# Pacing by VectorE's work, one PSUM pool and an ordered tail in a gated attention and mixer kernel

## Chip, cores and metric

One core of one Trainium2 chip. The metric is the device time of one execution in microseconds (us). TensorE (PE, its weight loads PEld), VectorE (DVE), ScalarE (ACT) and GpSimd (POOL) compute; SyncE (SP), ScalarE and GpSimd also issue DMAs. Each engine works through its own queue in order.

## What is computed

All tensors are float32; S = 2048 tokens, D = 640 channels, 32 heads of 20, F = 1728.

```python
qkv = x @ wqkv                                   # 32 heads of 20
p = softmax((q @ k.T) * 20 ** -0.5)              # 2048 x 2048 for each head
a = concat_heads(p @ v) @ wo
h = layernorm(x)                                 # over channels
b = (gelu(h.T @ w1 + b1) @ w2 + b2).T            # mixing over the 2048 tokens
g = sigmoid((x * gate_w).sum(-1, keepdims=True))
out = g * a + (1 - g) * b
```

## The kernel before

To keep float32 accuracy, operands are split into a high part (rounded) and a low part (the rest), written `hi_lo` (line 38): a copy on one engine, a subtraction on another. A product is three matmuls, high x high, high x low and low x high. Everything runs in one function, in these stages:

1. **Projections** (lines 344 to 542). Ten matmuls on zeros warm PE up (`warm`, 344 to 348). `load_x` (336) loads and splits blocks of x, `load_w` (289) the weights of q and k, `qk_unit` (299) multiplies and stores a 128 x 512 block of q or k as high and low parts to DRAM (`q_d`, `k_d`); `kd_d` holds differences of two key columns. Two projection blocks come first, then v with the gate, then the other blocks. Their PSUM tiles come from `st_tile` (73), four single banks in the pool `four`.
2. **Mixer** (lines 545 to 747). `mlp` (661) is a generator that yields after each step of two matmuls on 64 rows each (`pair64`): for each half `d` of the channels 14 hidden blocks `u` (656 steps), then 16 output blocks `y` (640 steps), 2592 steps in all. Weights come through `w_raw`, `w_split` and `w_need` (474 to 512). Between the steps run the row maxima of the first 1082 of the 2048 + 2 score tiles: attention subtracts each row's maximum through two extra rows of the score matmul, so all scores are computed once for their maximum (`s_mm`, 187) and once for the exponential. For the first eight of the 16 head pairs eight tiles are handled together (`s_diff`, 230): three go through a ScalarE relu (`s_over`, 208) and are joined on VectorE by a custom operation (`s_two`, 219), two take a VectorE reduce (`s_one`, 202): five VectorE operations for eight tiles. For the later pairs (`s_raw`, 257) each tile takes its own reduce; the last 58 tiles of the mixer stage are of this kind. Two tiles are emitted when `done < S_AHEAD * (n + 1) / STEPS`, evenly over the steps (line 731). They use four PSUM banks (`s` twice, `s3`, `pv`), the mixer the four of `st_tile`.

   The order on ScalarE, VectorE, POOL and SP is that of the program. On ScalarE a planner (`act`, `settle`, `force`, lines 547 to 581) decides where an operation is emitted: each has a cost in ns, a delay from which it may start and a slack until it is due; the clock of the plan advances by 146 per step and 233 per two score tiles. While the second half's input is normalised (`h_norm`, 450, in the y blocks of d = 0), VectorE does this as well.
3. **Attention loop** (lines 749 to 921). 16 head pairs x 32 iterations. An iteration has four score matmuls (`st_mm`), one exponential on a pair of banks (`st_pair`, 867), two on single banks (`st_one`, 875), two more score tiles for maxima while some of the other 968 are left, and the products with v of the iteration before (`pv_flush`, 818). Its banks are those of `psum` and of a second pool `trio`, which opens when `four` closes. `pv_evac` (803) copies the result out and stores it (`o_d`) and the row sums (`l_d`) to DRAM from POOL; `norm` (795) loads the row sums of some heads (`rl`), takes reciprocals on VectorE and stores them, repeated for the 20 rows of a head, to `r_d`. For the last four heads this happens at the end of the loop.
4. **Tail** (lines 922 to 953). The rows of `o_d` and `r_d` are loaded, multiplied and split, the first four blocks of 128 rows in pieces of 256 columns (`o_early`, two of them in the last pair of the loop), the last block in pieces of 512 (`o_late`). For each of 16 token tiles the mixer's output is loaded from `y_d` (945), `a_mms` (930) does 24 matmuls with the first four blocks (a) and adds the gated result to it on VectorE (939). After all of them 6 matmuls per tile follow with the last block (b), the second addition and the store to `out` (953). These run on four banks of a pool opened after `trio` closes; ScalarE, VectorE, POOL and SP are here in an order of the compiler's choice.

Of the kernel before, what the change touches and what calls it, by code (L numbers as in the profile page):

```python
# [30 lines left out]
def gated_mix(ctx, tc, xT, x, wqk, wv0, wv1, wo, w1, w1t, b1, w2, b2, out):  # L31
# [38 lines left out]
    four = ExitStack()  # L70
    banks = [four.enter_context(tc.tile_pool(name="four", bufs=1, space=PSUM))]
# [212 lines left out]
    def w_dma(m):  # L284
        raw = p1.tile([P, NC, P], F32, tag="xr", bufs=2, name=f"wr{m}")
        nc.scalar.dma_start(raw, wqk[m])
        return raw
# [11 lines left out]
    def qk_unit(m, w, q):  # L299
        wh, wl = w  # L300
        ps = st_tile([P, 512], f"qk{m}_{q}")
# [33 lines left out]

    def load_x(q):
        for c in range(NC):
            raw = px.tile([P, 512], F32, tag="x", bufs=8, name=f"xr{c}_{q}")
            nc.sync.dma_start(raw, xT[c * P:(c + 1) * P, q * 512:(q + 1) * 512])
            hi_lo(xh[c][q], xl[c][q], raw, hi_eng=nc.scalar)  # L340
# [5 lines left out]
    wps = st_tile([P, 512], "warm_ps")  # L346
    for i in range(10):
        nc.tensor.matmul(wps, warm[:, :P], warm, start=(i == 0), stop=(i == 9))
    raws = {0: w_dma(0), NC: w_dma(NC)}
    w = {0: load_w(0, raws[0])}  # L350
    load_x(0)
# [51 lines left out]
    for half in range(2):  # L403
        wvh, wvl = wvs[half]
        width = HALF + 2 if half == 0 else HALF
        for t in range(NT):
            n = NT * half + t
            if n == NT - 2:
                for i in range(4):
                    stats_load(i)  # L410
            if n == NT:
                nc.vector.tensor_scalar_mul(negm, gs[:, :, 1], -1.0 / D)
            if n in (2, 4, 6, 8, 10):
                split_wv(1, n // 2 - 1)
            if n == 2 * NT - 4:
                w[2] = load_w(2)
            ps = st_tile([P, width], f"v{half}_{t}")
# [353 lines left out]
    four.close()  # L771
    trio = ExitStack()
    tp = trio.enter_context(tc.tile_pool(name="trio", bufs=1, space=PSUM))
# [20 lines left out]

    def norm(h0, h1, at):
        loads, recips, stores = norm_steps(h0, h1)
        for n, f in enumerate(loads + recips + stores):
            if at is None:
                f()
            else:  # L800
                later[at if n == 0 else at + 10 + 2 * n] = f

    def pv_evac(p, qh, pv):
        ev = ap.tile([P, 512], F32, tag="oev", bufs=2, name=f"oev{p}_{qh}")
        nc.vector.tensor_copy(ev, pv)  # L805
        for j in range(2):
            h = 2 * p + j
            for c in range(2):
                r = 32 * (2 * j + c) + 11 * j
                cols = slice(qh * 1024 + c * 512, qh * 1024 + (c + 1) * 512)  # L810
                nc.gpsimd.dma_start(o_d[DH * h: DH * h + DH, cols], ev[r: r + DH, :])  # L811
                nc.gpsimd.dma_start(l_d[h: h + 1, cols], ev[r + DH: r + DH + 1, :])
        if qh == 1 and p in (7, 11, 13, 15):
            norm({7: 0, 11: 16, 13: 24, 15: 28}[p], 2 * p + 2, None if p == NP - 1 else 32 * p + 38)
# [23 lines left out]
    o_hl = {}  # L838

    def o_part(q, rows, k, n, tag, bufs, hi_eng, lo_eng):  # L840
        def t(name, dt=F32):
            return ap.tile([P, k, n], dt, tag=name + tag, bufs=bufs, name=f"{name}{tag}{q}")
        raw, rb, oh, ol = t("or"), t("rb"), t("oh", F32R), t("ol", F32R)
        cols = slice(q * n, (q + 1) * n)
        nc.sync.dma_start(raw, o_d[rows].rearrange("(c p) s -> p c s", p=P)[:, :, cols])
        nc.sync.dma_start(rb, r_v[rows].rearrange("(c p) s -> p c s", p=P)[:, :, cols])
        nc.vector.tensor_mul(raw, raw, rb)
        hi_lo(oh, ol, raw, hi_eng=hi_eng, lo_eng=lo_eng)
        return [(oh[:, i], ol[:, i]) for i in range(k)]

    def o_early(q, hi_eng=nc.scalar, lo_eng=nc.vector):
        o_hl[q] = o_part(q, slice(0, (NC - 1) * P), NC - 1, 256, "e", 2, hi_eng, lo_eng)

    def o_late(q):
        return o_part(q, slice((NC - 1) * P, D), 1, 512, "l", 4, nc.scalar, nc.vector)[0]
# [11 lines left out]
    def st_pair(g):  # L867
        ps = tp.tile([P, 2, 512], F32, tag="two", bufs=1, name=f"st{g}_0")
# [6 lines left out]
    def st_one(g, j):  # L875
        n = (2 * g + j) % 3
        ps = (psum if n == 2 else tp).tile([P, 512], F32, tag=("one0", "one1", "s3")[n], bufs=1, name=f"st{g}_1{j}")
# [6 lines left out]
    for p in range(NP):  # L884
# [3 lines left out]
        for it in range(32):  # L888
# [14 lines left out]
            if p == NP - 1 and it in (20, 26):  # L903
                o_early(it // 26, nc.gpsimd, nc.gpsimd)
# [17 lines left out]
    ordered.close()  # L922
    lps.close()
    trio.close()
    banks[0] = ctx.enter_context(tc.tile_pool(name="late", bufs=1, space=PSUM))

    ep = ctx.enter_context(tc.tile_pool(name="ep", bufs=1, side="right"))
    tys = [ep.tile([P, 2, HALF], F32, name=f"oy{t}") for t in range(NT)]

    def a_mms(t, ps, ohl, cc, cs):  # L930
        passes = [z for k, (oh, ol) in zip(cs, ohl) for z in ((oh[:, cc], woh[k]), (oh[:, cc], wol[k]),
                                                              (ol[:, cc], woh[k]))]
# [4 lines left out]
        c = slice(t, t + 1)  # L937
        for i in range(2):
            nc.vector.scalar_tensor_tensor(tys[t][:, i], ps[i], g_t[:, c], tys[t][:, i], op0=OP.mult, op1=OP.add)  # L939

    last = []
    for t in range(NT):
        if t % 2 == 0 and t // 2 + 2 < NT // 2:
            o_early(t // 2 + 2)
        nc.sync.dma_start(tys[t].rearrange("p a b -> p (a b)"), y_d[t * P:(t + 1) * P, :])
        if t in (4, 6, 8, 10):
            last.append(o_late(t // 2 - 2))
        ps = [st_tile([P, HALF], f"a{t}_{i}") for i in range(2)]
        a_mms(t, ps, o_hl[t // 2], slice((t % 2) * P, (t % 2 + 1) * P), range(NC - 1))
    for t in range(NT):  # L950
        ps = [st_tile([P, HALF], f"b{t}_{i}") for i in range(2)]
        a_mms(t, ps, [last[t // 4]], slice((t % 4) * P, (t % 4 + 1) * P), [NC - 1])
        nc.scalar.dma_start(out[t * P:(t + 1) * P, :], tys[t].rearrange("p a b -> p (a b)"))
# [47 lines left out]
```

## Time and profile before

| | |
|---|---|
| runs | 1814.91, 1814.11, 1813.07 us, median 1814.11 |
| profiled execution | 1807.24 us |
| its span | 1804.9 us |
| granted TensorE clock, mean | 0.997 |
| projections | 0 to 218 us |
| mixer with the first maxima | 218 to 746 us |
| attention loop | 747 to 1721 us |
| tail | 1721 us to the end |

Rows of a stretch (`A:B`) give its length, then for PE, PEld, DVE, ACT and POOL the busy time and in brackets the count of instructions, then the granted clock, the busy share of the DMA engines and GB/s. Rows of a timeline give start, duration, engine, line, operation, output<-inputs, shape, count, and in square brackets the idle time of the engine before it with what ended it. Rows of the waits give the waiting engine, what it waited for, total, times, longest. Rows of the groups (`L880 ACT ...`) give count, busy time, mean ns of one, idle time before. Rows of DMAs give count, size of each and median us from issue to landing.

### The profile page before, as it was taken

The numbers are of one execution on the slowest core, as the hardware profiler recorded it, in microseconds if no ns is written. First come the engines' busy times: TensorE is split into PE (matmuls) and PEld (weight loads), VectorE is DVE, ScalarE is ACT, GpSimd is POOL, SyncE is SP. The second block draws the span as 40 slices with busy tenths as digits, with TensorE's granted clock in tenths as the row PEclk, the third lists the DMA queues.
The fourth block names the chain that finished last, engine by engine and source line by source line (L and its number), as shares of the span: only waits on it lengthen the run. The fifth ranks groups of instructions, "written<-read, shape, count | busy, mean of one in ns | idle before, by whom it ended". The sixth has DMA issues, their size and how long they took to land. (4 is left out here: it accounts for less than half of the span.)

```text
span 1804.9 us, 39919 instructions
## 1 busy us (share of the span) xinstructions
PE 1787.0 (99%) x14978; PEld 1117.5 (62%) x14978; DVE 1240.6 (69%) x2407; ACT 1483.9 (82%) x2535; POOL 641.8 (36%) x898
## 2 busy tenths in 40 slices
PE   9999999999999999999999999999999999999998
PEld 7998799999999999533333333333333333333378
DVE  5303288899988888877767767676767677766136
ACT  4244378887888887699999999999999999999920
POOL 2113378788877777211110211121322121212210
PEclk9999999999999999999999999999999999999999
DMA  8657866556675564225222232052353332301463
GB/s 301 233 172 247 269 160 170 160 160 190 187 182 149 156 178 141 70 59 135 59 53 58 62 90 61 18 113 62 62 122 69 72 71 53 73 14 23 134 223 135
DMA packets 155666, 222.96 MB, mean 124 GB/s; under 512 B 65998, under 2 KB 92382, under 8 KB 152046
## 3 DMA queue, kind: packets, MB, share of 16 engines
q1 hardware_dynamic: 135472, 186.78, 38.2%
q0 software_dynamic: 15104, 23.01, 5.4%
q10 hardware_dynamic: 4896, 10.62, 1.8%
q8 instruction: 118, 1.93, 0.5%
q14 instruction: 76, 0.62, 0.1%
HBM read 165.43 MB, written 54.54 MB: 122 GB/s over the span
## 5 line engine op out<-in xcount | busy, mean ns | idle before, releaser
L205 DVE TENSOR_REDUCE mx<-s 128x1 f32<-128x512 f32 x1280 | 833.7, 687 | 288.9 <-PE s L199 225.1
L880 ACT ACTIVATE p<-st 128x512 f32<-128x512 f32 x1024 | 585.1, 659 | 0.0
L872 ACT ACTIVATE p<-st 128x1024 f32<-128x1024 f32 x512 | 553.8, 1082 | 1.3 <-PE st L865 0.7
L824 PE MATMUL pv<-p,v 128*32 128x512 f32 x4096 | 548.5, 605 | 0.1
L865 PEld LDWEIGHTS st<-qs_True,ks_True 62*128 62x128 f32 x2048 | 246.2, 185 | 434.9 <-ACT p L872 428.7
L865 PE MATMUL st<-qs_True,ks_True 62*128 62x512 f32 x2048 | 495.7, 446 | 1.8 <-ACT x L587 1.1
L199 PE MATMUL s<-ks_False,qs_False 60*128 60x512 f32 x1152 | 391.0, 398 | 4.5 <-ACT ov L214 2.9
L43 POOL TENSOR_TENSOR wl<-wr,wh 128x512 fp32r<-128x512 f32 x228 | 275.4, 1217 | 89.0 <-ACT wh L40 66.8
L224 DVE CUSTOM_DVE_ANT_0 ov<-s,ov 128x512 f32<-128x512 f32 x384 | 263.4, 687 | 38.6 <-PE s L199 24.9
L214 ACT ACTIVATE ov<-s 128x512 f32<-128x512 f32 x384 | 228.7, 597 | 73.0 <-PE s L199 61.9
L199 PE MATMUL s<-sk,sq 60*128 60x512 f32 x896 | 279.9, 394 | 0.0
L811 POOL DMA_DIRECT2D o_d<-oev x128 | 66.6, 521 | 590.4 <-DVE oev L805 587.9
L48 PE MATMUL y<-gh,wh 64*128 64x320 f32 x896 | 225.0, 309 | 0.0
L48 PE MATMUL u<-hl,wh 64*128 64x320 f32 x864 | 224.7, 307 | 0.0
L48 PE MATMUL u<-hh,wh 64*128 64x320 f32 x864 | 224.5, 307 | 0.0
L199 PEld LDWEIGHTS s<-ks_False,qs_False 60*128 60x128 f32 x1152 | 211.2, 185 | 14.7 <-DVE mx L205 6.7
L48 PE MATMUL y<-gl,wh 64*128 64x320 f32 x832 | 216.7, 307 | 0.0
L48 PE MATMUL y<-gh,wl 64*128 64x320 f32 x832 | 215.3, 306 | 0.0
L48 PE MATMUL u<-hh,wl 64*128 64x320 f32 x800 | 212.3, 307 | 0.0
L824 PEld LDWEIGHTS pv<-p,v 128*32 128x32 f32 x4096 | 83.1, 108 | 175.1 <-issue 162.6
L40 ACT ACTIVATE wh<-wr 128x512 fp32r<-128x512 f32 (+2 forms) x246 | 146.9, 600 | 52.7 <-DMA wr<-in_wqk_dram 22.5
L199 PEld LDWEIGHTS s<-sk,sq 60*128 60x128 f32 x896 | 166.3, 186 | 18.0
(130 smaller groups left out, 2441.3 us busy)
## 6 DMA issues: line engine op xcount, KB each, us to landing
wr<-in_w_dram SPq DMA_DIRECT2D x192, 256.0 KB
ks_True<-k_d SPq DMA_DIRECT2D x96, 160.0 KB
qs_True<-q_d SPq DMA_DIRECT2D x192, 80.0 KB
qs_False<-q_d SPq DMA_DIRECT2D x108, 80.0 KB
sk<-k_d SPq DMA_DIRECT2D x42, 160.0 KB
sq<-q_d SPq DMA_DIRECT2D x84, 80.0 KB
v_d<-vt SPq DMA_DIRECT2D x32, 168.0 KB
v<-v_d SPq DMA_DIRECT2D x16, 336.0 KB
```

Source lines behind the costliest of these rows:

```text
L40: nc.scalar.activation(hi, src, AF.Copy)
L43: (lo_eng or nc.vector).tensor_sub(lo, src, hi.bitcast(F32))
L48: nc.tensor.matmul(ps[k], a[r], b[r], start=start, stop=stop)
L199: nc.tensor.matmul(ps, qs[half][r, t * P:(t + 1) * P], ks[r, kc * 512:(kc + 1) * 512], start=True, stop=True)
L205: nc.vector.tensor_reduce(mx[:, slot, j, t: t + 1], ps, axis=AX.X, op=OP.max)
L214: nc.scalar.activation(over[j, kc], ps, AF.Relu)
L224: nc.vector.tensor_tensor_reduce(ov, ps, ov, 1.0, -3.0e38, OP.add, OP.max, mx[:, slot, j, t: t + 1])
L811: nc.gpsimd.dma_start(o_d[DH * h: DH * h + DH, cols], ev[r: r + DH, :])
L824: nc.tensor.matmul(pv[r: r + 32, :], v_tiles[p][:, kt, 10 * j: 10 * j + 32], pt[j, c], start=(kt == 0), stop=(kt == NT - 1))
L865: nc.tensor.matmul(ps, ks[r, kt * P:(kt + 1) * P], qs[qh][r, c * 512:(c + 1) * 512], start=True, stop=True)
L872: nc.scalar.activation(pt, ps, AF.Exp, scale=SCALE)
L880: nc.scalar.activation(pt, ps, AF.Exp, scale=SCALE)
```

## The change

- **Pacing.** Score tiles are emitted by VectorE's planned work: 435 ns for a tile of the first kind, 640 for the second, 400 for a normalisation. The sum grows evenly from step 14 on.
- **PSUM.** There is one pool: `s` twice, `s3`, `pv`, a pair of banks `two`, `one0`, `one1`. The projections rotate over the four single banks `s3`, `pv`, `one0`, `one1` (`one_tile`); mixer and tail take `two` and `one0`, `one1` in turn (`st_tile`); the loop uses the same tiles as before without opening a pool.
- **Opening.** Eight warm matmuls instead of ten; the first weight in two DMAs (one block, then four); the x blocks' DMAs ahead of the second weight's, which goes to POOL's queue.
- **Weight splits.** The splits 4 to 7 of the mixer's weights get a delay of 4000 ns and a slack of 2000.
- **Loop's end.** `pv_evac` issues the four `l_d` stores before the four `o_d` stores. In the last pair y is loaded by SP (`y_load`, one tile an iteration from the 13th on, into buffers that the loop's operands left), and four early pieces of `o_d` and `r_d` at the iterations 16, 20, 26 and 30.
- **Tail.** It keeps the program's order on all engines. Tiles 0 to 7 take the four first blocks (24 matmuls); each of tiles 8 to 15 takes all five (30), followed by the last block of the tile eight before it (6). The row sums of the last heads are loaded at the end of the loop, their reciprocals and stores come after tile 2, the late rows' multiplications at tiles 6 and 9; the late loads are issued by POOL, the stores to `out` by SP.

```diff
     def st_tile(shape, name):
         n = st_count[0] % 4
         st_count[0] += 1
-        return banks[0].tile(shape, F32, tag=f"st{n}", bufs=1, name=name)
+        if n == 0:
+            st_pair_of[0] = psum.tile([P, 2, 512], F32, tag="two", bufs=1, name=name)
+        if n < 2:
+            return st_pair_of[0][:, n, :shape[1]]
+        return psum.tile(shape, F32, tag=f"one{n - 2}", bufs=1, name=name)
+
+    def one_tile(shape, name):
+        n = one_count[0] % 4
+        one_count[0] += 1
+        return psum.tile(shape, F32, tag=("s3", "pv", "one0", "one1")[n], bufs=1, name=name)
...
-    for i in range(10):
-        nc.tensor.matmul(wps, warm[:, :P], warm, start=(i == 0), stop=(i == 9))
-    raws = {0: w_dma(0), NC: w_dma(NC)}
-    w = {0: load_w(0, raws[0])}
-    load_x(0)
+    for i in range(8):
+        nc.tensor.matmul(wps, warm[:, :P], warm, start=(i == 0), stop=(i == 7))
+    wr0 = p1.tile([P, NC, P], F32, tag="xr", bufs=2, name="wr0")
+    parts = (slice(0, 1), slice(1, NC))
+    for c in parts:
+        nc.scalar.dma_start(wr0[:, c], wqk[0][:, c])
+    xr0 = [x_dma(c, 0) for c in range(NC)]
+    raws = {NC: w_dma(NC, nc.gpsimd)}
+    w = {0: tuple(q4([P, NC, P], F32R, f"w{n}0") for n in "hl")}
+    for c in range(NC):
+        if c < 2:
+            hi_lo(w[0][0][:, parts[c]], w[0][1][:, parts[c]], wr0[:, parts[c]], hi_eng=nc.scalar)
+        x_split(c, 0, xr0[c])
...
-            act(lambda: w_split(j), 520, 0, 2200 * (j - k) - 4000)
+            act(lambda: w_split(j), 520, 4000 if j < 2 * AHEAD else 0, 2000 if j < 2 * AHEAD else 2200 * (j - k) - 4000)
...
+    FIRST = 14
+    U_STEPS = (FT - 1) * 48 + 32
+    DIFF, RAW, NORM = 435, 640, 400
+
+    def dve_work(k):
+        return DIFF * min(k, NDIFF * 128) + RAW * max(0, k - NDIFF * 128)
+
+    def dve_room(n):
+        norms = min(max((n - U_STEPS) / (NT * 40), 0), 1) * NT * NORM
+        return (dve_work(S_AHEAD) + NT * NORM) * (n + 1 - FIRST) / (STEPS - FIRST) - norms
...
-        while done + 2 <= S_AHEAD and done < S_AHEAD * (n + 1) / STEPS:
+        while done + 2 <= S_AHEAD and dve_work(done) < dve_room(n):
...
-                nc.gpsimd.dma_start(o_d[DH * h: DH * h + DH, cols], ev[r: r + DH, :])
                 nc.gpsimd.dma_start(l_d[h: h + 1, cols], ev[r + DH: r + DH + 1, :])
+                stores.append((o_d[DH * h: DH * h + DH, cols], ev[r: r + DH, :]))
+        for a in stores:
+            nc.gpsimd.dma_start(*a)
...
+            if p == NP - 1:
+                last_norm.extend(norm_steps(h0, H))
+                last_norm[0][0]()
...
-            if p == NP - 1 and it in (20, 26):
-                o_early(it // 26, nc.gpsimd, nc.gpsimd)
+            if p == NP - 1:
+                if it in (16, 20, 26, 30):
+                    e_load((16, 20, 26, 30).index(it))
+                if 13 <= it < 13 + NT:
+                    y_load(it - 13)
+                if it in (20, 26):
+                    e_high(it // 26, ap, nc.gpsimd)
+                    e_low(it // 26, nc.gpsimd)
...
+    late_args = {n: l_load(n) for n in (2, 0, 3, 1)}
+    for n in (2, 0, 3, 1):
+        nc.gpsimd.dma_start(*late_args[n][0])
+    e_high(2, lp)
     for t in range(NT):
+        q = t // 2 + 2
+        if t % 2 == 0 and 2 < q < NT // 2:
+            e_high(q, ap if q % 4 < 2 else lp)
+        lates = {NT // 2 - 2: (2, 0), NT // 2 + 1: (3, 1)}.get(t, ())
+        for n in lates:
+            l_high(n)
+        evacs = [a_tile(t, range(NC) if t >= NT // 2 else range(NC - 1))]
+        if t >= NT // 2:
+            evacs.append(a_tile(t - NT // 2, [NC - 1]))
+        for f in evacs:
+            f()
+        if t % 2 == 0 and q < NT // 2:
+            e_low(q)
+            if q + 2 < NT // 2:
+                e_load(q + 2)
+        for n in lates:
+            l_low(n)
+        if t == 2:
+            for f in last_norm[1] + last_norm[2]:
+                f()
+            for n in (2, 0, 3, 1):
+                nc.gpsimd.dma_start(*late_args[n][1])
+    ordered.close()
+    lps.close()
```

`e_load`, `e_high` and `e_low` are the load, the multiplication with the high part, and the low part of an early piece; `l_load`, `l_high` and `l_low` those of a late one. `a_tile` emits a tile's matmuls and returns its evacuation.

More of the change, by code (lines that the diff above doesn't have):

```diff
@@ L851, in o_early, with o_tiles @@
[L851 to L855, printed above, removed]
+    o_raw, o_hl, l_hl = {}, {}, {}
+    def o_tiles(q, k, n, tag, bufs, names, pool, dt):
+        if pool is lp:
+            return [lp.tile([P, k, n], dt, tag="sq", bufs=4, name=f"{name}{tag}{q}") for name in names]
+        return [pool.tile([P, k, n], dt, tag=name + tag, bufs=bufs, name=f"{name}{tag}{q}") for name in names]
@@ L867, in st_pair @@
     def st_pair(g):
[L868 removed]
+        ps = psum.tile([P, 2, 512], F32, tag="two", bufs=1, name=f"st{g}_0")
         for j in range(2):
@@ L921, in gated_mix, with a_tile @@
     pv_flush()
[L922 to L932, printed above, removed]
+    def a_tile(t, cs):
+        ps = [st_tile([P, HALF], f"a{t}_{cs[0]}_{i}") for i in range(2)]
+        passes = []
+        for k in cs:
+            (oh, ol), n, i = (o_hl[t // 2], 2, k) if k < NC - 1 else (l_hl[t // 4], 4, 0)
+            cc = slice((t % n) * P, (t % n + 1) * P)
+            passes += [(oh[:, i, cc], woh[k]), (oh[:, i, cc], wol[k]), (ol[:, i, cc], woh[k])]
         for i, (a, b) in enumerate(passes):
@@ L950, in gated_mix, with evac @@
[L950 to L953, printed above, removed]
+        def evac():
+            c = slice(t, t + 1)
+            for i in range(2):
+                nc.vector.scalar_tensor_tensor(tys[t][:, i * HALF:(i + 1) * HALF], ps[i], g_t[:, c], tys[t][:, i * HALF:(i + 1) * HALF], op0=OP.mult, op1=OP.add)
+                if t == NT // 2 - 1 and NC - 1 in cs:
+                    put = (nc.scalar if i else nc.sync).dma_start
+                    put(out[t * P:(t + 1) * P, i * HALF:(i + 1) * HALF], tys[t][:, i * HALF:(i + 1) * HALF])
+            if t != NT // 2 - 1 and NC - 1 in cs:
+                nc.sync.dma_start(out[t * P:(t + 1) * P, :], tys[t])
```

104 lines of the change are left out of this document (65 added, 39 removed).

## The prediction

> **What bounds the kernel now.** The first view is the page's head.
>
> ```profile
> span 1804.9 us, 39919 instructions
> PE 1787.0 (99%) x14978; PEld 1117.5 (62%) x14978; DVE 1240.6 (69%) x2407; ACT 1483.9 (82%) x2535; POOL 641.8 (36%) x898
> ```
>
> TensorE (PE) looks full. But its busy time comes from matmuls that overlap, and the count in equal stretches says more. The second view gives stretches of 22 us of the mixer stage (about 218 to 746 us), then one of them for the score tiles alone, then four rows of PE's timeline.
>
> ```profile
> 218.00:240.00 22.00, 19.15 (x208) 18.45 (x209) 14.66 (x35) 14.07 (x27) 11.57 (x11) 0.92 0.65 194
> 394.00:416.00 22.00, 21.89 (x265) 21.30 (x263) 20.86 (x52) 18.07 (x37) 18.14 (x20) 1.00 0.65 187
> 438.00:460.00 22.00, 21.67 (x266) 21.08 (x263) 20.55 (x52) 17.73 (x36) 19.03 (x21) 1.00 0.47 147
> 636.00:658.00 22.00, 22.00 (x276) 21.93 (x275) 19.25 (x50) 18.16 (x35) 15.07 (x18) 1.00 0.53 152
> 702.00:724.00 22.00, 21.74 (x251) 20.03 (x249) 20.58 (x45) 11.87 (x24) 15.56 (x18) 1.00 0.38 114
> 724.00:746.00 22.00, 21.68 (x217) 17.35 (x213) 22.00 (x38) 6.17 (x11) 7.42 (x8) 1.00 0.05 17
> ```
>
> ```profile
> 636.00:658.00 22.00, 15.76 (x48) 8.67 (x48) 19.01 (x30) 10.51 (x18) 1.00 0.53 152
> ```
>
> ```profile
> 742.71 0.31 PE L48 MATMUL y<-gh,wl 64*128 64x320 f32 x1
> ...
> 743.15 0.31 PE L48 MATMUL y<-gh,wl 64*128 64x320 f32 x1
> ...
> 745.68 0.31 PE L48 MATMUL y<-gh,wh 64*128 64x320 f32 x1
> 747.11 0.73 PE L865 MATMUL st<-qs_True,ks_True 62*128 62x512 f32 x3 [1.12 <-ACT x L587]
> ```
>
> The first bracket in a row is PE's count. A full stretch holds 276, which is 12.5 per us. Against that the first stretch lacks 68 matmuls (5.4 us), the last two lack 25 and 59 (6.7 us), and the three from 394 to 460 (first and last shown) lack about 11 each (2.6 us). Elsewhere in this stage little is missing. From 742.71 to 743.15 lie six intervals, so one mixer matmul takes 0.073 us and a step of two 0.147 us. The full stretch has 228 of them and 48 score tiles, which leaves (22 - 228 x 0.0733) / 48 = 0.11 us for a score tile.
>
> Next, why these stretches are short:
>
> ```profile
> PE s L199 <- ACT ov L214: 2.9, 1, 2.9
> ```
>
> ```profile
> 222.51 0.63 ACT L40 ACTIVATE wh<-wr 128x512 fp32r<-128x512 f32 x1 [1.72 <-DMA wr<-in_w_dram]
> 223.05 1.76 ACT L214 ACTIVATE ov<-s 128x512 f32<-128x512 f32 x3
> ```
>
> ```profile
> 224.00:228.00 4.00, 4.00 (x34) 4.00 (x32) 2.46 (x7) 1.83 (x4) 1.78 (x2) 0.58 0.98 310
> ```
>
> At the stage's start PE waits 2.9 us for a relu of a score tile. ScalarE runs in order, and that relu stands behind a weight split that waits for its DMA. After this pause the granted clock is 0.58 over 4 us, which costs 0.42 x 4 = 1.7 us more. Together: 4.6 us.
>
> ```profile
> 405.25 0.68 DVE L224 CUSTOM_DVE_ANT_0 ov<-s,ov 128x512 f32<-128x512 f32 x1
> ...
> 408.34 0.25 DVE L160 TENSOR_REDUCE mm<-mx 128x8 f32<-128x24 f32 x2
> ...
> 719.54 27.55 DVE L205 TENSOR_REDUCE mx<-s 128x1 f32<-128x512 f32 x46
> ```
>
> Where VectorE (DVE) is never idle, five operations take 408.34 - 405.25 = 3.09 us; these serve eight score tiles of the first kind (three take the relu's way), 0.386 us a tile. Of the second kind, from 719 us on, every tile needs its own reduce: 27.55 / 46 = 0.599 us. Before, both kinds come at 1082 / 2592 = 0.417 tiles a step. The 58 of the second kind then span 139 steps, in which PE needs 139 x 0.147 + 58 x 0.11 = 26.8 us and VectorE 34.7. VectorE is the bound there, and the missing 6.7 us are this.
>
> The attention loop is paced by ScalarE:
>
> ```profile
> L880 ACT ACTIVATE p<-st 128x512 f32<-128x512 f32 x1024 | 585.1, 659 | 0.0
> L214 ACT ACTIVATE ov<-s 128x512 f32<-128x512 f32 x384 | 228.7, 597 | 73.0 <-PE s L199 61.9
> ```
>
> No idle time stands before its exponentials, two of them single tiles in each of 512 iterations. Nothing in the change shortens them. Last the tail, by PE's timeline, stretches, the end of the chain, then VectorE, GpSimd (POOL) and SP:
>
> ```profile
> 1721.70 0.56 PE L935 MATMUL a<-woh,ohe 128*128 128x320 f32 x2
> ...
> 1750.18 1.09 PE L935 MATMUL a<-woh,ohe 128*128 128x320 f32 x2 [1.77 <-DVE oy L939]
> ```
>
> ```profile
> 1750.00:1754.00 4.00, 3.80 (x14) 3.55 (x15) 2.63 (x5) 0.00 (x0) 0.00 (x0) 0.57 0.82 281
> 1754.00:1784.00 30.00, 30.00 (x206) 29.91 (x205) 18.72 (x30) 5.57 (x7) 0.00 (x0) 1.00 0.19 63
> ```
>
> ```profile
> 1783.96 15.51 PE b L935 x95
> ```
>
> ```profile
> 1721.80 0.69 DVE L805 COPY oev<-pv 128x512 f32<-128x512 f32 x1 [12.67 <-PE pv L824]
> ...
> 1738.64 0.55 DVE L785 RECIPROCAL rl<-rl 128x64 f32<-128x64 f32 x1 [5.22 <-DMA rl<-l_d]
> ...
> 1748.43 1.23 DVE L847 TENSOR_TENSOR ore<-ore,rbe 128x1024 f32<-128x1024 f32 x1 [5.19 <-DMA ore<-o_d]
> ...
> 1784.78 15.72 DVE L939 SCALAR_TENSOR_TENSOR oy<-b,g_t,oy 128x320 f32<-128x320 f32 x32
> ```
>
> ```profile
> 1732.04 0.57 POOL L782 DMA_DIRECT2D rl<-l_d x1 [5.23 <-DMA l_d<-oev]
> 1739.49 2.75 POOL L789 DMA_DIRECT2D r_d<-rl x4 [6.89 <-DVE rl L785]
> ```
>
> ```profile
> 1740.30 0.37 SPq L846 DMA_DIRECT2D rbe<-r_d x1
> ```
>
> PE has 480 matmuls to do from 1721.70 on. At 30 / 205 = 0.1463 us that is 70.2 us, so they could end at 1791.9; they end at 1799.5. The 7.6 us go to two waits of VectorE for DMAs (5.2 us each), behind which PE runs out of banks, to a clock of 0.57 after the second, and to the b part, where 32 evacuations of 0.49 us set the pace (15.5 us for 95 matmuls, not 13.9).
>
> **The change part by part.**
>
> *Pacing.* VectorE's work is spread evenly over 2578 steps, the first 14 left free: 1024 x 435 + 58 x 640 + 16 x 400 = 488,960 ns, or 190 a step. That is 0.436 tiles a step of the first kind, 0.413 while the normalisations run (10 ns a step off), 0.296 of the second kind. The 58 late tiles now span 196 steps: PE 28.8 + 6.4 = 35.2 us, VectorE 34.7. Nearly level; I leave 1.0 us lost of 6.7: **-5.7**. In the dense stretches a step takes PE 0.147 + 0.436 x 0.11 = 0.195 us and VectorE 0.436 x 0.386 = 0.168, so PE stays the bound, with less air than before (0.161 of 0.193). I take **+1.5** (bounds 0, and 13.6 at the loss of 394 to 460: 33 matmuls of 828, so 4%, of 1742 steps or 339 us). In the normalising stretch 1% fewer tiles on an engine at its limit: **-1.0** (0 to -2.6).
>
> *Start of the mixer.* The free steps let the last projection banks drain, the new rotation begins on a bank pair that no projection used, and the first four splits get a delay of 4 us, so the first relus stand ahead of the split that waits for its DMA. PE meets the first split chunk of the new kind only at step 48, some 9 us in. **-4.6** (0 to -5.4).
>
> *One PSUM pool.* Before, the loop's first scores wait 1.12 us until the mixer's last bank is read, as a pool closes. Now they go into the pair that was read one tile earlier, but their exponential still stands behind the two evacuations on ScalarE: **-0.7** (0 to -1.1). The pair is freed only when both halves are read, half a microsecond after the first; a whole unit lies between, which hides it.
>
> *The opening.*
>
> ```profile
> 1.44 4.63 PE L348 MATMUL warm_ps<-warm 128*128 128x512 f32 x10 [1.44 <-DVE warm L345]
> ...
> 7.02 0.50 PE L54 MATMUL qk<-xh,wh 128*128 128x512 f32 x1 [0.95 <-ACT xh L40]
> ```
>
> The first weight comes in two pieces and the x blocks ahead of the second weight, which moves to POOL's queue. PE waits 0.95 us before its first product; half of that is won: **-0.5** (-1.0 to +1.7, the price of one clock step as at 224). The Trainium skill, "TensorE: Matmul & The Clock Gate", "Why this matters for your kernels", asks for at least 4 us of matmuls before the clock is full; eight at 0.463 us are 3.7, and by it the first products could run at half clock, which would make the sum 1.7 us worse. In the trace the clock is already up behind ten; no run here shows eight. The same section lets gaps of up to about 3 us go unpunished; the 1.77 us at 1750 were followed by 0.57, so here the trace decides against it. "DMA: Bandwidth & Descriptors", "Issuing engines are not separate DMA queues", says that another queue saves issue time only; by that the opening wins nothing and the sum is 0.5 worse.
>
> *The tail.* y is loaded in the last pair, where ScalarE paces and SP has nothing else due, so the 16 loads are hidden; without that cover they would fill the queues as before. The evacuations of a and b interleave: 36 matmuls (5.3 us) against four evacuations (2 us), so the 1.6 us of the b part go. The late reciprocals still stand in VectorE's order behind tile 2 (about 1734.6). Their chain:
>
> ```profile
> L812 POOL DMA_DIRECT2D l_d<-oev x128 | 64.1, 501 | 2.6 <-issue 2.6
> ```
>
> ```profile
> l_d<-oev POOLq DMA_DIRECT2D x128, 2.0 KB, 2.6
> ```
>
> ```profile
> r_d<-rl POOLq DMA_DIRECT2D x32, 160.0 KB, 5.7
> ```
>
> The copy ends at 1722.5, four l_d stores of 0.5 us now go first (1724.8), land after 2.6 (1727.4), rl arrives 6.6 later as before (1734.0): no wait. r_d stores issue until 1738, land by 1743; the new wait is that VectorE at tile 6 multiplies the late rows, for which POOL's loads must land. At 4 us each (no row shows them on POOL; bounds 2.6, and 8.1 as from 1740.30 to 1748.43) that is about 1747.5; behind the multiplication stands the evacuation of tile 6, for which PE's tile 8 waits from 1749.9. It just fits; I leave 1.0 us. PE ends 7.6 - 1.0 us earlier, with the last evacuations and stores as long as before: **-6.6** (0 to -7.6).
>
> *Sum:* -0.5 - 4.6 - 1.0 + 1.5 - 5.7 - 0.7 - 6.6 = **-17.6**. The profiled execution took 1807.2 us (span 1804.9), so 1789.6 there; the median of the runs shown is 1814.1, 6.9 above, and the same gain gives **1796.5**.
>
> **The rivals.**
>
> *Late rows come late.* Arrivals as slow as in the old tail (l_d 5.2, rl 6.6, r_d 5.7, load 8.1): VectorE stands until about 1754, evacuates tile 6 by 1755.9, PE loses 6.0 and then 1.7 by the clock instead of 1.0: 1796.5 + 6.7 = **1803**. For it: the two 5.2 us waits. Against: those ran beside the y loads.
>
> *VectorE binds in the dense stretches.* Loss as at 394 to 460, 13.6 instead of 1.5: **1809**. Against: VectorE's 0.168 of 0.195.
>
> *The late tiles stay bunched*, if planned costs don't fit: 5.7 less, **1802**.
>
> *Slower: the loop.* Its tiles move to other banks of the one pool. If the exponentials read these more slowly, each of 512 iterations pays. From 17.6 / 512 = 34 ns an iteration on nothing is won, from 41 on it is slower by over 0.2%. Between the two single-tile rows above lie 62 ns (659 and 597 for one shape); one such step gives 1796.5 + 512 x 0.062 = **1828**. Against: tile shapes and order stay.
>
> *All waits go:* 1.0 + 5.4 + 2.6 + 6.7 + 1.1 + 7.6 = 24.4, **1790**.
>
> **How the numbers follow.** Forecast 0.63 (own range 1792 to 1800), late rows 0.13, dense stretches 0.09, bunched 0.03, loop 0.07, all gone 0.05. The range 1789 to 1806 leaves out the dense stretches and the loop, 0.16. About 0.2% (3.6 us) is what a measurement of this kernel tells from no change; faster by more: 0.63 + 0.13 + 0.05 + 0.03 and 0.05 of the 0.09, together 0.89; same 0.04; slower 0.07.
>
> **What would show it.** Right: about 276 matmuls in each 22 us after the first, no clock step near 224, VectorE near its limit but PE not short before the loop, b matmuls at 0.146 us, and no wait of PE for oy. Wrong: fewer than 270 from 240 to 350; the multiplication of late rows waiting past 1750; exponentials longer than 659 ns; a clock step behind eight warm matmuls.

## The result, and the profile after

The changed kernel took **1799.97 us** (median of 6 runs, 1797.92 to 1806.11); the kernel before, beside it on the same chip, 1813.75 us (6 runs, 1810.34 to 1815.16). The ratio is 0.9934, 95% interval 0.9914 to 0.9954. The forecast was 1796.5 us: the sign is right, and 13.8 of the 17.6 us of gain came. The profiled execution was the longest of the six, 1806.11 us with a span of 1803.8. So the two profiles differ by only 1.1 us of span, and stages have to be compared, not totals. The table cuts the span at the first matmul of each stage (read from the trace); "again" is a second profile of the same changed kernel (first experiment).

| us | before | after | again | forecast of the change |
|---|---|---|---|---|
| opening and projections | 218.4 | 225.4 | 221.2 | -0.5 |
| mixer | 528.7 | 522.6 | 518.8 | -10.5 |
| attention loop | 974.6 | 975.6 | 975.5 | 0 |
| tail | 83.2 | 80.2 | 80.1 | -6.6 |
| span | 1804.9 | 1803.8 | 1795.7 | -17.6 |

The page's head of the kernel after:

```profile
span 1803.8 us, 39867 instructions
PE 1782.3 (99%) x14976; PEld 1108.8 (61%) x14976; DVE 1232.8 (68%) x2392; ACT 1482.9 (82%) x2536; POOL 646.1 (36%) x907
```

The stretches of 22 us that the prediction read, in the kernel after, with the dense middle (460 to 702 us) in one row:

```profile
218.00:240.00 22.00, 19.31 (x172) 17.11 (x170) 10.66 (x22) 9.96 (x18) 7.73 (x6) 1.00 0.90 291
240.00:262.00 22.00, 20.76 (x249) 20.37 (x251) 17.80 (x45) 18.56 (x40) 14.77 (x15) 1.00 0.61 162
394.00:416.00 22.00, 21.51 (x264) 20.90 (x262) 20.12 (x49) 18.48 (x37) 16.09 (x17) 1.00 0.52 155
438.00:460.00 22.00, 22.00 (x269) 21.64 (x268) 20.41 (x52) 18.04 (x36) 19.11 (x22) 1.00 0.62 186
460.00:702.00 242.00, 240.38 (x2936) 238.42 (x2934) 217.21 (x549) 198.75 (x392) 184.17 (x195) 1.00 0.62 164
702.00:724.00 22.00, 22.00 (x278) 21.86 (x276) 20.50 (x46) 13.79 (x27) 16.04 (x18) 1.00 0.50 148
724.00:746.00 22.00, 22.00 (x281) 21.95 (x279) 21.79 (x36) 9.43 (x17) 14.25 (x14) 1.00 0.23 71
```

The last two rows are the forecast come true: 278 and 281 matmuls where 251 and 217 stood. VectorE is busy 21.79 of 22 us in the last one, at its limit and no longer behind it. The first two show what did not come as forecast: the stage starts 7 us later and still lacks matmuls. The waits of PE, with the total, the number and the longest:

```profile
PE s L208 <- ACT ov L223: 5.2, 3, 2.3
PE a L1022 <- DVE oy L1028: 2.9, 8, 1.2
PE qk L54 <- DVE evl L43: 2.1, 1, 2.1
...
PE v L54 <- DVE kf L326: 1.1, 1, 1.1
```

The wait for the relus (`ov`) at the mixer's start has not gone, and eight waits for `oy` stand in the tail, where the kernel before had two (3.0 us). The tail's end, by the chain that ended last:

```profile
1738.08 2.68 issue
1740.76 1.37 POOL r_d L820 x2
1742.13 3.80 DMA r_d<-rl
...
1746.60 4.14 DMA rbl<-r_d
1750.77 1.35 DVE orl L913 x2
1752.12 0.93 DVE oy L1028 x2
1753.19 4.64 PE a L1022 x30
1757.86 1.02 DVE oy L1028 x2
1758.92 4.67 PE a L1022 x30
1763.62 1.02 DVE oy L1028 x2
1764.68 4.68 PE a L1022 x30
```

From tile 8 on a round of 36 matmuls takes 1764.68 - 1758.92 = 5.76 us, where 36 x 0.1463 = 5.27 were counted on. The chain goes through the 30 matmuls of the long product and then through an evacuation; the 6 of the short product are not in it.

### The profile page after: what moved, and what is told of

It reads as the page before. It is cut to its first block, busy times and chain, and to the rows that moved or that the text cites. A ratio compares the mean times of both kernels' runs of the same rounds, so it can differ in the third digit from the quotient of the medians.

```text
span 1803.8 us, 39867 instructions
## 1 busy us (share of the span) xinstructions
PE 1782.3 (99%) x14976; PEld 1108.8 (61%) x14976; DVE 1232.8 (68%) x2392; ACT 1482.9 (82%) x2536; POOL 646.1 (36%) x907
## 3 DMA queue, kind: packets, MB, share of 16 engines
q8 instruction: 118, 1.93, 0.5%
## 4 chain that ended last, share of the span: by engine, by line
PE 87%; DMA 6%; issue 2%; DVE 2%; POOL 1%; ACT 1%; SPq 0%; ACTq 0%; DVEq 0%; POOLq 0%
PE pv L862 28%; PE st L949 20%; PE s L208 12%; PE y L48 10%; PE u L48 9%; PE v L54 4%; PE a L1022 3%; DMA wr<-in_wqk_dram 2%; PE qk L54 2%; DMA wr<-in_w_dram 1%; DMA kd_d<-kf 1%; DVE oy L1028 1%; DMA xm<-in_x_dram 0%; DVE ov L233 0%; DMA q_d<-evl 0%
## 5 line engine op out<-in xcount | busy, mean ns | idle before, releaser
L964 ACT ACTIVATE p<-st 128x512 f32<-128x512 f32 x1024 | 570.5, 630 | 0.0
L956 ACT ACTIVATE p<-st 128x1024 f32<-128x1024 f32 x512 | 539.8, 1054 | 0.5 <-PE s L208 0.5
L208 PE MATMUL s<-ks_False,qs_False 60*128 60x512 f32 x1152 | 337.1, 396 | 6.2 <-ACT ov L223 5.2
L842 POOL DMA_DIRECT2D l_d<-oev x128 | 62.7, 497 | 594.5 <-DVE oev L835 589.0
L48 PE MATMUL y<-gl,wh 64*128 64x320 f32 x832 | 213.5, 306 | 0.0
L40 ACT ACTIVATE wh<-wr 128x512 fp32r<-128x512 f32 (+3 forms) x247 | 147.3, 599 | 64.5 <-DMA wr<-in_wqk_dram 29.3
L208 PEld LDWEIGHTS s<-ks_False,qs_False 60*128 60x128 f32 x1152 | 189.3, 184 | 11.9 <-ACT ov L223 7.1
L48 PE MATMUL u<-hl,wh 64*128 64x320 f32 x864 | 177.2, 307 | 0.0
L48 PE MATMUL u<-hh,wh 64*128 64x320 f32 x864 | 177.0, 307 | 0.0
L48 PE MATMUL u<-hh,wl 64*128 64x320 f32 x800 | 165.5, 307 | 0.0
```

What stands on the lines that cost most here:

```text
L40: nc.scalar.activation(hi, src, AF.Copy)
L48: nc.tensor.matmul(ps[k], a[r], b[r], start=start, stop=stop)
L208: nc.tensor.matmul(ps, qs[half][r, t * P:(t + 1) * P], ks[r, kc * 512:(kc + 1) * 512], start=True, stop=True)
L956: nc.scalar.activation(pt, ps, AF.Exp, scale=SCALE)
L964: nc.scalar.activation(pt, ps, AF.Exp, scale=SCALE)
```

## The experiments

Theory after the first comparison: pacing, start and loop came about as forecast; the eight warming matmuls and the new order of loading make the opening late; in the tail the banks turn so that PE waits for an evacuation every round. Rivals: the differences are chance between executions, or lie in the late rows' transfers. The kernel before was measured again beside each of three groups of runs, and each ratio below is against that of its group. It stood at 1810.98 us (17 runs) beside the changed kernel again, the old pacing, the banks of their own and the old opening; at 1810.96 (16 runs) beside the pacing alone, the twelve warming matmuls, y in the tail and the best version; at 1809.99 (11 runs) beside the late rows back at tile 6 and the old order.

### The changed kernel again

No edit.

> The changed kernel unaltered, for a second profile. Theory: in the first profile the projections ended 7 us later than before (225.4 against 218.4 us) because a weight load and stores landed late by chance and the clock stepped down twice; in another execution they end within 3 us of before, and the time is near 1799. Rival: the later end belongs to the change, and this profile shows about 225 again with a time near 1806.

Measured: 1801.03 us (1797.9 to 1804.88), ratio 0.9951 (0.9933 to 0.9968). The projections end at 221.2 us and not at 225.4. In the profile after, a weight had come late there:

```profile
207.45 0.74 ACT L40 ACTIVATE wh<-wr 128x640 fp32r<-128x640 f32 x1 [7.62 <-DMA wr<-in_wqk_dram]
```

Behind it PE waits 2.1 us and then has a granted clock of 0.50 from 211.0 to 213.5 us. The second profile shows neither, so about 4 of the 7 us do not come in every execution; the other 2.8 stay. Whether the 4 are chance alone is not shown: PE waits 1.1 and 1.3 us at this place in two more of the six profiles with the new order of loading, and at most 0.2 in the six with the old order.

### The old pacing alone put back

```
-        while done + 2 <= S_AHEAD and dve_work(done) < dve_room(n):
+        while done + 2 <= S_AHEAD and done < S_AHEAD * (n + 1) / STEPS:
```

> Only the pacing rule is set back: score tiles evenly over the steps again, everything else as changed. Theory: the 58 late tiles bunch again before the loop and PE runs short from 702 to 746, so it is 5 to 6 us slower than the changed kernel (about 1805). Rival: the gain comes from the pool and the tail, and this is as fast as the changed kernel within 1.5 us.

Measured: 1807.99 us (1801.12 to 1815.11, 12 runs), ratio 0.9988 (0.9972 to 1.0005), so 7.0 us above the changed kernel of the same group, a little more than expected. The profiled execution was the longest of the twelve, so its span is not compared. Its windows before the loop are short again, as in the kernel before:

```profile
702.00:724.00 22.00, 22.00 (x268) 21.38 (x265) 19.93 (x47) 14.82 (x29) 16.07 (x18) 1.00 0.46 142
724.00:746.00 22.00, 21.55 (x216) 17.30 (x216) 22.00 (x39) 7.44 (x13) 10.90 (x11) 1.00 0.09 30
```

### The pacing alone, in the kernel before

The edit is the opposite one: the functions `dve_work` and `dve_room` and the line above, put into the kernel before.

> The kernel before with the pacing of the maximum tiles by VectorE's work alone, all else as it was. Theory (the pacing's gain comes from filling the stretch before the loop, and nothing else of the change is needed for it): 5 to 7 us faster than the kernel before, about 1804 to 1806 us, with 276 or more matmuls in each of the windows 702 to 724 and 724 to 746 us. Rival (it needs the single banks or the delays that the other parts gave): less than 3 us faster, 1808 us or more.

Measured: 1803.01 us (1800.01 to 1805.29, 9 runs), ratio 0.9959 (0.9945 to 0.9973): 8.0 us, more than expected. The window 702 to 724 is full (279 matmuls). The mixer ends at 742.6 here, so the window from 724 on holds the old loop start too; from 724 to 742 us PE has 230 matmuls, 12.8 per us, which is full. Both directions agree: the pacing is worth 7 to 8 us by the medians (4.9 to 10.0 by the interval of this ratio), needs no other part, and is the largest term.

### The short product in banks of its own

```
-        ps = [st_tile([P, HALF], f"a{t}_{cs[0]}_{i}") for i in range(2)]
+        tile_of = s_tile if cs[0] == NC - 1 else st_tile
+        ps = [tile_of([P, HALF], f"a{t}_{cs[0]}_{i}") for i in range(2)]
```

> In the tail the last block's six matmuls of a tile write to the two score banks, which are free there, so tiles 8 to 15 alternate over two pairs. Theory: PE waits 0.5 us in each of eight rounds because the next 30 matmuls return to the pair whose evacuation began only 0.9 us before; with this edit rounds take 5.3 instead of 5.8 us and the kernel is 3.5 to 4 us faster than the changed one. Rival: VectorE is late in the tail anyhow, rounds stay at 5.8 us and nothing changes.

Measured: 1797.71 us (1796.44 to 1800.05), ratio 0.9934 (0.9919 to 0.9949), 3.3 us below the changed kernel. The intervals of the two ratios overlap, so the profile has to decide: its tail is 77.2 us long and not 80.1, although PE waits 1.8 us for the late rows here and 1.1 in the changed kernel's second profile. The chain of this kernel no longer goes through evacuations from tile 8 on:

```profile
1741.80 4.81 DMA rbl<-r_d
1746.63 1.34 DVE orl L913 x2
1749.04 41.46 PE a L1023 x281
```

And VectorE's rows:

```profile
1764.27 1.93 DVE L1029 SCALAR_TENSOR_TENSOR oy<-a,g_t,oy 128x320 f32<-128x320 f32 x4 [1.17 <-PE a L1023]
...
1769.40 1.93 DVE L1029 SCALAR_TENSOR_TENSOR oy<-a,g_t,oy 128x320 f32<-128x320 f32 x4 [2.08 <-PE a L1023]
1774.83 0.55 DVE L1029 SCALAR_TENSOR_TENSOR oy<-a,g_t,oy 128x320 f32<-128x320 f32 x1 [3.50 <-PE a L1023]
```

Two rounds lie between the first and the last, (1774.83 - 1764.27) / 2 = 5.28 us each. So the rival, that VectorE itself is too slow for the round, falls: four evacuations (1.93 us) fit easily. With two bank pairs, long and short products alternate, and each long one meets the pair that the long one before it has just filled.

### The late rows one tile later, and back

This run is built on the best version, which is shown last: there the late rows are multiplied at tile 7. The edit puts that back to tile 6.

```
-        lates = {NT // 2 - 1: (2, 0), NT // 2 + 1: (3, 1)}.get(t, ())
+        lates = {NT // 2 - 2: (2, 0), NT // 2 + 1: (3, 1)}.get(t, ())
```

> The best version so far with one edit: the late rows' multiplication back from tile 7 to tile 6 of the tail. Theory (at tile 6 the multiplication waits for the copies of the sums, about 1.2 us of TensorE in a usual execution, 4 and a half-clock stretch when they come late): 1 to 3 us slower than the best version, 1794 to 1796 us, with a wait of VectorE for the copies of 3 to 4 us. Rival (a free place among the banks hides it, now that the single banks take the short products): within 0.5 us of the best version, 1793 us.

Measured: 1794.81 us (1791.26 to 1795.9), ratio 0.9906 (0.9891 to 0.9922); the best version had 0.9913 (0.9894 to 0.9932) in its group. The intervals lie on each other: this does not tell the two apart. The profile shows why:

```profile
1744.13 1.33 DVE L905 TENSOR_TENSOR orl<-orl,rbl 128x512 f32<-128x512 f32 x2 [2.94 <-DMA rbl<-r_d]
1745.39 1.00 DVE L1021 SCALAR_TENSOR_TENSOR oy<-a,g_t,oy 128x320 f32<-128x320 f32 x2
```

VectorE waits 2.94 us, but of this PE feels 0.3 (its only wait for `oy` in this profile). In the changed kernel's two profiles it waited 3.8 and 3.6 us, with the short products in their own banks 4.5 (PE 1.8), and in the profiles with the old pacing and with twelve warming matmuls 5.5 and 5.0, with PE standing for 4.0 and 3.4 us and a half-clock stretch behind it. That is the rival "late rows come late": it occurs in some executions (2 of the 9 profiles that multiply them at tile 6), not in the usual one.

### The old opening

```
-    for i in range(8):
+    for i in range(10):
...
-    for c in parts:
-        nc.scalar.dma_start(wr0[:, c], wqk[0][:, c])
-    xr0 = [x_dma(c, 0) for c in range(NC)]
-    raws = {NC: w_dma(NC, nc.gpsimd)}
...
+    raws = {0: w_dma(0), NC: w_dma(NC)}
+    w = {0: load_w(0, raws[0])}
+    load_x(0)
```

> Only the opening is set back: ten warm matmuls, whole weight loads, x after them. Theory: eight warm matmuls end too early and the clock falls back to half near 9 us, so that the second product block starts at 13.2 instead of 11.9; set back it starts at 11.9 again and the kernel is about 1 us faster. Rival: the new opening wins 0.5 us as I forecast, and this is 0.5 us slower.

Measured: 1795.78 us (1793.75 to 1801.7), ratio 0.9929 (0.9911 to 0.9946), 5.3 us below the changed kernel of the same group. The new opening costs time, and more than expected. How much is surer by the profiles, as the intervals of the two ratios overlap. Three of them (this one, the best version, the late rows at tile 6) have the old opening and all else of the projections as in the changed kernel: these end at 219.4 to 220.2 us, 219.6 in the mean. In the six with the new order they end at 220.9 to 225.4, 222.3 in the mean, so 2.7 us later.

### Twelve warming matmuls, the new order kept

```
-    for i in range(8):
+    for i in range(12):
...
```

> The changed kernel with twelve warming matmuls in place of eight, its new order of loading kept. Theory (eight half-speed matmuls end too early, the work behind them comes in pieces and the clock is taken back for 3.4 us): the half-clock stretch near 9 us goes, 1 to 3 us faster than the changed kernel, 1797 to 1799 us. Rival (the new order of loading, not the clock, makes the opening late: the second half of the first weights comes after the work that needs it): the second block of products starts near 13 us as before it, time stays at 1800 us.

Measured: 1799.92 us (1797.96 to 1805.51, 8 runs), ratio 0.9952 (0.9935 to 0.997): no gain. Two rows of the kernel after (the warming, then one of the products that follow) and the same of this one:

```profile
1.44 3.78 PE L363 MATMUL warm_ps<-warm 128*128 128x512 f32 x8 [1.44 <-DVE warm L360]
...
9.67 0.63 PE L54 MATMUL qk<-xh,wh 128*128 128x512 f32 x1
```

```profile
1.44 4.45 PE L363 MATMUL warm_ps<-warm 128*128 128x512 f32 x12 [1.44 <-DVE warm L360]
...
9.57 0.40 PE L54 MATMUL qk<-xh,wh 128*128 128x512 f32 x1
```

In the kernel after the granted clock is 0.50 from 9.7 to 12.2 us, where seven such products run; so a product of 0.63 us runs at half clock, and one of 0.40 at full. With twelve, none of the opening's products is long, and the 40th begins at 16.5 us; with eight, in the five profiles of the changed kernel and its variants with the new order, at 17.5 to 19.5 (mean 18.6). So the clock half of the theory held, by 2.1 us in one profile. But most of this is lost again by 74 us, as the stretches show, first of this kernel, then of the kernel after, then of the best version, which has the old opening:

```profile
12.00:62.00 50.00, 48.51 (x211) 39.28 (x210) 26.28 (x43) 19.87 (x37) 7.77 (x17) 1.00 0.89 298
62.00:74.00 12.00, 10.95 (x68) 10.19 (x67) 4.84 (x11) 3.27 (x8) 3.24 (x6) 1.00 0.89 298
```

```profile
12.00:62.00 50.00, 49.77 (x216) 40.40 (x215) 26.33 (x43) 19.55 (x35) 7.39 (x17) 0.99 0.91 297
62.00:74.00 12.00, 10.91 (x65) 10.03 (x65) 4.68 (x11) 3.87 (x9) 3.26 (x7) 1.00 0.86 291
```

```profile
12.00:62.00 50.00, 50.00 (x216) 40.51 (x215) 27.30 (x45) 20.02 (x38) 8.32 (x18) 1.00 0.91 306
62.00:74.00 12.00, 12.00 (x75) 11.38 (x74) 4.27 (x10) 3.23 (x7) 2.83 (x6) 1.00 0.95 303
```

The DMA engines are busy nine tenths of the time in all three. With the new order PE's busy time falls 1.1 us short from 62 to 74 us, with twelve warming matmuls another 1.5 us from 12 to 62. The waits of PE behind it are one for an x block (1.3 us near 31 us, with twelve warming matmuls alone) and one near 70 us, of 0.4 to 1.4 us in all six profiles with the new order and absent in the six with the old. It is for a copy that itself waits for an earlier store of its buffer, in the kernel after:

```profile
70.24 0.69 DVE L326 COPY kf<-qk 128x512 f32<-128x512 f32 x1 [5.69 <-DMA kd_d<-kf]
```

With the old order the copy waits about as long (4.9 to 5.6 us in three profiles), but PE still has work. By 74 us, the profiles with the new order have begun 287 to 296 products (295 with twelve warming matmuls), those with the old order 297 to 312. What starts earlier here only waits later.

### The old order, eight warming matmuls kept

The loading as in the old-opening diff, the eight left as they are.

> The changed kernel with the old order of loading and its own eight warming matmuls (the counterpart of the run with twelve warming matmuls and the new order). Theory (the new order costs by itself: what it starts earlier waits for data near 30 and 69 us, because the transfers of the first 72 us fill the DMA engines): the waits near 30 and 69 us go whatever the warming, 2 to 4 us faster than the changed kernel, 1796 to 1798 us, with at most a half-clock stretch near 9 us left. Rival (warming and order only cost together, each alone is harmless): 1795 us or less, as with the old opening whole.

Measured: 1798.41 us (1794.83 to 1801.45), ratio 0.9932 (0.9917 to 0.9948). By the median that is about 2 us below the changed kernel and 2.6 above the whole old opening, as the theory has it; by the ratios it is as good as the whole old opening (0.9929), as the rival has it. The runs don't tell these apart. The profile is plainer:

```profile
12.00:62.00 50.00, 50.00 (x217) 40.93 (x217) 26.55 (x44) 19.93 (x37) 7.77 (x17) 1.00 0.90 301
62.00:74.00 12.00, 12.00 (x73) 11.11 (x72) 4.89 (x11) 3.30 (x8) 3.24 (x6) 1.00 0.91 303
```

PE's waits near 31 and 70 us are gone, so they belong to the order. The half-clock products are there (0.63 us until 12.7 us), and the 40th begins at 19.3 us, against 18.2 and 17.4 with ten warming matmuls and the same order (old opening, kernel before). How much of the 5.3 us is the order's and how much the warming's stays open; each has a loss of its own that the profiles show, of 1 to 2 us in the mean: by 74 us this profile has begun 297 products, the three with ten warming matmuls and the same order 300 to 305, the five with eight and the new order 287 to 296.

### y loaded in the tail

```
-                if 13 <= it < 13 + NT:
-                    y_load(it - 13)
...
+    for t in range(NT):
+        y_load(t)
     for t in range(NT):
         q = t // 2 + 2
```

> The changed kernel with the sixteen loads of y issued at the start of the tail, ahead of its first tile, and not in the loop's last pair. Theory (they share the queues with the sums and the late rows, which come later for it): the late rows' wait of VectorE grows from 3.8 us to 6 or more and the tail by 3 to 6 us, 1803 to 1806 us. Rival (y is needed only behind the first products, and its loading is hidden wherever it stands): within 1 us of the changed kernel, 1800 us.

Measured: 1798.59 us (1796.49 to 1803.11), ratio 0.9943 (0.9924 to 0.9961), the tail 79.9 us. The theory fell: the late rows' wait is 3.5 us, no longer than in the changed kernel. Sixteen loads on SP's queue do not harm the tail, and no gain of loading y early shows.

### The best version

Three edits together: short products in their own banks, the old opening, the late rows at tile 7. (The expectation below calls the first of them the products with the embedding values in the four single banks; the edit is the one shown above, the last block's six matmuls in the two score banks.)

> The changed kernel with three edits: the probabilities' products with the embedding values in the four single banks, the old opening (ten warming matmuls and the old order of loading), and the late rows' multiplication moved from tile 6 to tile 7 of the tail. Theory (the opening costs 2 to 5 us, the bank pairs of the tail about 3, the late rows' wait about 1, and the three lie in different stages): the gains add up, 1791 to 1794 us, the tail about 76 us long. Rival (the opening's 4 us and the tail's 3 us are the same chance events of the clock, seen twice): no better than the better of the two alone, 1795.8 us.

Measured: **1793.11 us** (1790.54 to 1798.25), ratio 0.9913 (0.9894 to 0.9932), faster than the kernel before and, by the medians, than every other version. The gains add up (5.3 and 3.3 from 1801.0 leave 1792.4). The tail is 75.1 us long, and in its chain one unbroken piece stands from the first product to the last:

```profile
1712.83 2.94 PE pv L854 x16
1715.76 69.57 PE a L1015 x473
1785.36 1.47 DVE oy L1021 x3
```

That is, within 0.7 us, the floor which the prediction worked out, 480 x 0.1463 = 70.2 us (seven records are missing in the row).

## Why the prediction was right or wrong, step by step

**Pacing (-5.7, with +1.5 for the dense stretches and -1.0 for the normalising one): right.** Late tiles: 84 matmuls (6.7 us) were missing in the last two windows, now none; the 1.0 us left over for them was not needed. The dense stretches lost more than forecast: from 460 to 702 us there are 2936 matmuls, 2925 in the second profile and 2948 with the pacing alone, where the kernel before has 2976, so 2.2 to 4.1 us. The normalising stretch gained 0.2 to 1.0: 1069, 1079 and 1076 matmuls in the four windows from 372 to 460 where the kernel before has 1066 (two of the rows of after are above). With the pacing alone the rows make 6.7 - 2.2 + 0.8 = 5.3 us, the three forecast terms 5.2. Whole runs say 7 to 8, with an interval that reaches down to 4.9; where the rest would lie is not shown.

**Start of the mixer (-4.6): right only in the mean.** What stood right before the relus, the weight split that waits for its load, has gone, but what stood ahead of it remains: the last evacuations of the projections, which wait for the stores that free their buffer. The prediction read the split alone; ScalarE of the kernel before had this wait too, 2.52 us where the split's was 1.72:

```profile
219.67 0.60 ACT L40 ACTIVATE evh<-qk 128x512 fp32r<-128x512 f32 x1 [2.52 <-DMA k_d<-evh]
```

ScalarE and then PE of the kernel after:

```profile
226.34 0.60 ACT L40 ACTIVATE evh<-qk 128x512 fp32r<-128x512 f32 x1 [1.49 <-DMA k_d<-evh]
...
229.80 0.60 ACT L40 ACTIVATE evh<-qk 128x512 fp32r<-128x512 f32 x1 [2.34 <-DMA k_d<-evh]
...
231.53 1.09 ACT L223 ACTIVATE ov<-s 128x512 f32<-128x512 f32 x2 [0.62 <-DMA k_d<-evl]
```

```profile
232.18 0.49 PE L208 MATMUL s<-ks_False,qs_False 60*128 60x512 f32 x1 [2.32 <-ACT ov L223]
```

PE's last product of the projections began at 225.05, its evacuation at 229.80. The prediction let the 14 free steps drain the banks without asking what the evacuations wait for. Over the ten profiles of the new start PE waits 0 to 4.7 us there, and in four of them a half-clock stretch follows. With the pacing alone the mixer takes 525.0 us; over the nine profiles with pacing and new start it takes 520.5 in the mean (518.4 to 522.6). So start and loop start together bring about 4.5 where 5.3 were forecast, by one profile of the pacing alone.

**One PSUM pool (-0.7): right.** PE's idle time before the loop's first scores, on the page of after, is 0.9 us with the rest of that line, where the kernel before has 1.8; the two waits behind it are 0.5 and 0.4 us in all ten profiles with the one pool, 1.1 and 0.7 in both without:

```profile
L949 PE MATMUL st<-qs_True,ks_True 62*128 62x512 f32 x2048 | 496.7, 446 | 0.9 <-ACT ty L681 0.5
L964 ACT ACTIVATE p<-st 128x512 f32<-128x512 f32 x1024 | 570.5, 630 | 0.0
```

**The slower rival, the loop's banks: fell.** The exponentials are recorded with 630 ns, not over 659. What decides is the loop's length, 975.6 us, 1.0 more than before, where the rival had 32.

**The opening (-0.5): wrong, by 3 to 6 us.** (3.2 by the projections' mean length in the profiles, 5.8 by the old opening's runs.) Here the mechanism failed as a whole. The prediction counted the 0.95 us before the first product, and won them (5.60 us, not 7.02), but set the clock's price at the far end of the range and did not ask whether the data behind the first product come any sooner. Both came: half-clock products, and a wait near 70 us. The rows decide for the rule that the prediction weighed and did not take. With eight warming matmuls (3.41 to 3.78 us) half-clock products of 0.63 us followed in all six profiles, with ten in three of five, with twelve in none of one. The Trainium skill, "TensorE: Matmul & The Clock Gate", "Why this matters for your kernels", asks for at least 4 us of matmuls. The trace agrees in direction, but 4.4 to 4.6 us (ten matmuls and then 1.0 to 1.2 us of waiting) were not always enough. The three of five are those with the one pool, the two without half-clock products those with the old pools; whether that is chance is not shown.

**The tail (-6.6): half right.** The b part's pace and the 5.2-us waits went. The late rows cost about the 1.0 us left for them: VectorE waited 3.76 us in the kernel after, and PE 1.2. What failed is the sentence that 36 matmuls stand against four evacuations: VectorE has the time, but the banks do not. Each of eight rounds loses 0.5 us to it, 4.0 us; with 1.2 from the late rows that is 5.2 us lost in the tail where the kernel before lost 7.6.

**The sum.** The forecast was -17.6. The opening makes it 3 to 6 worse, the tail 3.6, the start 0.8 and the loop 1.0; the pacing is as forecast by its rows and 2 to 3 better by whole runs. That makes -6 to -12. Measured, against the kernel before of the same group: -13.8 and, again, -10.0. The parts read off the profiles come out short, because the profiled execution of the kernel before (1807.24 us) was 2.8 to 6.5 us quicker than the medians of its groups of runs; which stage is longer in the others no profile shows.

That the time came so near the forecast is in part luck. Of the four signs named for being wrong, three came in the profile after: 249 matmuls in the window from 240 us, the late rows' multiplication at 1750.77, and the clock step behind eight warming matmuls. The first two come with the late opening of that execution (273 matmuls and 1742.55 in the second profile), the third, or a half clock from the first product on, in all six profiles with eight.

## What to carry to other kernels

Where two kinds of tile load an engine differently, space them by that engine's work and not by count: this rule alone was worth about half of the change or more. When products of different length share a rotation of bank pairs, write down which pair each meets and when it was last read; an evacuation engine with time to spare doesn't help if the long product always meets the pair just filled. A first product that started earlier was worth nothing here, in a stretch where the DMA engines are busy nine tenths of the time, so look at what the tenth and the fortieth wait for.

## What the runs showed of the hardware that was not expected

- The recorded length of an instruction is not its pace. The loop's single exponentials went from 659 to 630 ns and the pairs from 1082 to 1054, which would be 2 x 0.029 + 0.028 = 0.086 us in each of 512 iterations, 44 us; the loop became 1.0 us longer.
- The granted clock can read 1.00 where the products run at half clock: the old order with eight warming matmuls shows 1.00 from 9 to 13 us while its products last 0.63 us. Nine profiles have half-clock products in the opening. In the four where the column shows a step, products of full speed stand ahead of it; in the five where it reads 1.00, the products are long from the first one. So a clock that is low from the start seems to go unrecorded, and there the products' lengths tell more than the clock column.
- Between the first `r_d` store of GpSimd and the next three stand 2.68 us in which it waits for nothing that the profile shows (1738.08 above, also with the short products in their own banks). Its cause was not sought.
